# A range test and a guarded general path behind an attention and maxout kernel

## The chip, the cores and the metric

The kernel runs on one core of one Trainium2 chip. The metric is the time of one execution on the device, in microseconds (us). A core has five engines that run side by side, each with its own list of instructions: TensorE (PE in the profile; PEld are its weight loads), VectorE (DVE), ScalarE (ACT), GpSimd (POOL) and SyncE (SP), which issues most DMA transfers. They wait for each other through semaphores.

## The reference

Attention over 8 batches, 8 heads, 1152 keys and 64 dimensions, with queries pooled by two, and behind it a layer of two products whose maximum is taken.

```python
q_pool = q.reshape(B, H, S // 2, 2, D).mean(axis=3)
scores = scale * np.matmul(q_pool, k.transpose(0, 1, 3, 2))
scores = scores - np.max(scores, axis=-1, keepdims=True)
attn = np.exp(scores)
attn = attn / (np.sum(attn, axis=-1, keepdims=True) + 1e-09)
attn_out = np.matmul(attn, v)

x = attn_out.transpose(0, 2, 1, 3).reshape(B * 576, 512)
h1 = x @ w1                       # 512 x 1024
h2 = x @ w2                       # 512 x 1024
out = np.maximum(h1, h2) @ w_out  # 1024 x 512
```

q, k and v are drawn from a normal distribution times 0.1.

## The kernel before

The work is cut into 32 pairs of heads (four pairs a batch). For each pair, q, k and v are loaded in fp32 and cast to bf16 (GpSimd), q and k are transposed, and TensorE makes the scores in groups of 2 x 512 columns into PSUM. ScalarE takes the exponential without subtracting a row maximum and writes `et` in bf16. TensorE multiplies by v, which carries a column of ones, so that column 64 of each result holds the softmax sum. `norm` (line 517) takes the reciprocals of those sums on VectorE, into one of two small tiles `rc` (five columns for the first head of a pair, four for the second), and multiplies the results by them (lines 521 and 525) into `xnat`. After a transposition the rows stand in `xT`.

The maximum is computed as max(h1 - h2, 0) + h2: the weights' difference `wd` and the product `w21` of w2 and w_out are made once. `h_jobs` multiplies xT by wd, with a maximum with zero on the way out of PSUM (lines 778 and 782); `p_job` sums the products with w21 and w_out (line 864), and the result is copied to `osb` by ScalarE or VectorE in turn (lines 891 and 894; 876 and 880 for the last block, which is cut in two) and stored by SyncE and ScalarE (line 735; `store_pair`, lines 745 and 751, earlier).

A planner lays out all operations with costs, then `reorder` puts the lists of TensorE, VectorE, GpSimd and SyncE into orders that are written out by hand as strings, one letter an operation (`pe_order`, `dve_order`, `pool_order`, `sp_order`). `solve` works out which semaphore each operation waits for: an operation counts up its engine's semaphore only if another needs it. `emit` writes each engine's list in that order (line 197 issues the waits). So an operation that waits holds up everything behind it on its engine.

At the end, SyncE waits for the last stores (line 204), and leaving the block (profile line 249) drains every engine and joins them in a barrier. Nothing follows.

Of the kernel before, what the change touches and what calls it, by code (L numbers as in the profile page):

```python
# [1 line left out]

# [2 lines left out]

FP32 = mybir.dt.float32
BF16 = mybir.dt.bfloat16
P = 128

EXP = mybir.ActivationFunctionType.Exp  # L10
RELU = mybir.ActivationFunctionType.Relu
COPY = mybir.ActivationFunctionType.Copy
ALU = mybir.AluOpType
AX = mybir.AxisListType


class Plan:
# [75 lines left out]
    def lane(self, o):  # L93
        key = (o["w"] or ("o",))[0]
        if o["eng"] == "PE":
            return "S" if key[0] == "s" else key[1:]
        if o["eng"] == "SP":
            return {"kT": "t"}.get(key[:2], key[0])
        if o["eng"] == "POOL":
            return {"kb": "k", "wd": "d"}.get(key[:2], key[0])  # L100
        for k in o["r"] + o["w"]:
            if k[0] == "f" and k[1:].isdigit():
                return k[1:]
        return {"qt": "T", "w2": "W", "wo": "W"}.get(key[:2], "Q")

    def reorder(self, want):

# [37 lines left out]
    def solve(self):  # L145
        ops = self.ops
        know = {}
        dma_seen = {}
        for n, o in enumerate(ops):
            eng = o["eng"]  # L150
            kn = know.setdefault(eng, {})
            o["waits"] = []
            for d in sorted(o["deps"], reverse=True):
                p = ops[d]
                if p["dma"] is None:
                    if p["eng"] == eng and not o["fence"] and (eng == "PE" or eng != "DVE" and d not in o["raw"]):
# [12 lines left out]
            if o["dma"] is not None:  # L169
                dma_seen[o["dma"]] = dma_seen.get(o["dma"], 0) + 1  # L170
                o["count"] = 16 * dma_seen[o["dma"]]
        need = set()
        for o in ops:
            need.update(o["waits"])
        cnt = {}
        for n, o in enumerate(ops):
            if o["dma"] is None:
                o["inc"] = n in need
                if o["inc"]:
                    cnt[o["eng"]] = cnt.get(o["eng"], 0) + 1  # L180
                    o["count"] = cnt[o["eng"]]
        self.dma_total = {k: 16 * v for k, v in dma_seen.items()}
# [30 lines left out]
        self.single = single  # L213


def bass_funnel_attn__then__act_maxout2_kernel(
    nc: bass.Bass,
    q: bass.AP,
# [19 lines left out]
    NC_ = C // P  # L238
    NF = F // P
# [9 lines left out]
    with ctx:  # L249
        def sbuf(shape, dt, name):  # L250
            return ctx.enter_context(nc.sbuf_tensor(name, list(shape), dt))
# [3 lines left out]

        ident = sbuf([P, P], BF16, "ident")
        qraw = [sbuf([P, QU, 2, D], FP32, f"qraw{s}") for s in range(3)]
# [147 lines left out]
        def dve(fn, r, w, cost):  # L405
            op("DVE", fn, r=r, w=w, cost=cost)
# [73 lines left out]
        def av_jobs(i):  # L480
            b, h0 = i // NHP, 2 * (i % NHP)
            es = i % 2
            vs = i % 3
            xs = b % 2
            need = [f"et{es}.{g - first(i)}" for g in range(first(i), after(i))] + [f"vE{vs}", f"v.{i}"]

            def col(half, t, sb):
                return (half * 2 + es) * PW + flat(i, t, sb * P)

            def chunk(half, sb):  # L490

                def go(e, m):
                    for t in range(NT):
                        a = col(half, t, sb)
                        last = e.matmul(  # L495
                            fb[m][:, sb * 66:sb * 66 + 65], et[:, a:a + P],
                            vE[vs][:, t, half, 0:65], start=(t == 0), stop=(t == NT - 1))
                    return last
                return unit(need, 0.2755, go)

            def rest():

                def go(e, m):
                    for t in range(NT):
                        for half in range(2):
                            a = col(half, t, NCH)
                            last = e.matmul(  # L507
                                fb[m][rows(half), NCH * 66:NCH * 66 + 65], et[:, a:a + NB],
                                vE[vs][:, t, half, 0:65], start=(t == 0), stop=(t == NT - 1))
                    return last  # L510
                return unit(need, 0.308, go, "c")

            def norm(half):
                def evac(m):
                    n = NCH + 1 - half
                    a = fb[m][:, 0:(NCH + 1) * 66].rearrange("p (j c) -> p j c", c=66)
                    dve(lambda e: e.reciprocal(rc[half][:, 0:n], a[:, 0:n, 64:65]),  # L517
                        [f"f{m}"], [f"rc{half}"], 0.19)
                    if half == 0:
                        for k in range(2):  # L520
                            dve(lambda e, k=k: e.tensor_tensor(
                                xnat[xs][rows(0), i % NHP, NCH, k * D:k * D + D], a[rows(k), NCH, 0:D],
                                rc[0][rows(k), NCH:NCH + 1].to_broadcast([HP, D]), ALU.mult),
                                [f"f{m}", "rc0"], [f"xr{xs}.{h0 + k}"], 0.221)
                    dve(lambda e: e.tensor_tensor(
                        xnat[xs][:, i % NHP, 0:NCH, half * D:half * D + D], a[:, 0:NCH, 0:D],
                        rc[half][:, 0:NCH].unsqueeze(2).to_broadcast([P, NCH, D]), ALU.mult),
                        [f"f{m}", f"rc{half}"], [f"xn{xs}.{h0 + half}", f"f{m}"], 0.425)
# [847 lines left out]
        while p_end[0] < NTOK:  # L1376
# [69 lines left out]
        plan.solve()  # L1446
        engines, dmas = plan.sems()
        sem = {n: ctx.enter_context(nc.semaphore("sem_" + n)) for n in engines + dmas}
        block = ctx.enter_context(nc.Block())

        @block.gpsimd
        def _(g):
            plan.emit("POOL", g, sem)

        @block.sync
        def _(sp):
            plan.emit("SP", sp, sem, last_waits=[f"d_o{s}" for s in range(4)] + [f"d_z{s}" for s in range(4)])

        @block.vector
        def _(vc):  # L1460
            plan.emit("DVE", vc, sem)

        @block.scalar
        def _(ac):
            plan.emit("ACT", ac, sem)

        @block.tensor
        def _(pe):
            plan.emit("PE", pe, sem)


# [26 lines left out]
```

## Time and profile before

| | |
|---|---|
| median of 3 runs | 367.25 us (365.64 to 368.3) |
| profiled execution | span of 368.9 us, from the first to the last instruction; the page gives no separate time for it |
| TensorE busy | 359.1 us of the span |
| mean granted TensorE clock | 0.984 |
| HBM read, written | 62.91 MB, 9.44 MB |

All times in the profile are of that one execution. A group's row gives the engine's line, the operation, what it writes and reads, the count, then busy time and the mean duration in ns, and behind the second bar the engine's idle time before it and what ended that. A letter q behind an engine's name means its sequencer: waits, branches, drains and DMA issues, which don't count as busy.

### The profile page before, as it was taken

What the parts mean: (1) busy time and instruction counts of PE and PEld (TensorE: products, weight loads), DVE (VectorE), ACT (ScalarE), POOL (GpSimd) and SP (SyncE); (2) the same over time, 40 slices, a digit from 0 to 9 for tenths busy, and PEclk for the clock granted to TensorE, in tenths of its full rate; (3) what the DMA queues carried; (4) which work ended last, traced back from release to release, by engine and by line L of the source; (5) the groups of instructions that cost most, each with busy time, mean ns of one, the idle gap of its engine ahead of it and who ended that gap; (6) DMA issues with size and microseconds to landing.
All of it is one profiled execution on the core that took longest, in us unless ns stands there. A gap on an engine that the chain in (4) does not pass through costs nothing.

```text
span 368.9 us, 13316 instructions
## 1 busy us (share of the span) xinstructions
PE 359.1 (97%) x5941; PEld 225.9 (61%) x5945; DVE 240.9 (65%) x521; ACT 315.6 (86%) x355; POOL 124.7 (34%) x111
## 2 busy tenths in 40 slices
PE   6999999999999999999999999999999999999996
PEld 5766564665556665657565665665666666556853
DVE  1478378867778867848885776577877766714411
ACT  4699989999999998999998999999999989895221
POOL 1256675533134333372242602525224440010000
PEclk9599999999999999999999999999999999999999
DMA  7999959999939998898999999998999680913206
GB/s 265 406 396 397 402 108 328 307 312 164 330 102 234 291 271 253 211 297 178 251 349 185 252 245 236 283 304 181 277 253 197 191 201 6 181 43 72 54 0 171
DMA packets 77640, 84.71 MB, mean 230 GB/s; under 512 B 49936, under 2 KB 50704, under 8 KB 77584
## 3 DMA queue, kind: packets, MB, share of 16 engines
q1 hardware_dynamic: 77024, 83.09, 84.8%
q8 instruction: 46, 0.75, 0.9%
q10 hardware_dynamic: 560, 0.79, 0.6%
q14 instruction: 10, 0.08, 0.1%
HBM read 62.91 MB, written 9.44 MB: 196 GB/s over the span
## 4 chain that ended last, share of the span: by engine, by line
PE 95%; DMA 2%; ACT 2%; issue 1%; SPq 0%; POOL 0%; DVE 0%; DVEq 0%
PE sps L584 22%; PE sps L495 12%; PE sps L831 11%; PE fb L831 10%; PE fb L495 9%; PE sps L798 8%; PE fb L798 7%; PE sps L864 3%; PE sps L507 2%; PE fb L716 2%; DMA kraw<-in_k_dram 2%; ACT et L591 2%; PE fb L507 1%; PE fb L864 1%; PE sps L771 1%; PE fb L319 1%
## 5 line engine op out<-in xcount | busy, mean ns | idle before, releaser
L591 ACT ACTIVATE et<-sps 128x1024 bf16<-128x1024 f32 (+1 forms) x336 | 307.6, 1002 | 25.1 <-PE sps L584 23.0
L584 PE MATMUL sps<-qpT,kT 64*128 64x256 bf16 (+7 forms) x1162 | 121.5, 287 | 1.0 <-issue 0.5
L449 DVE STREAM_TRANSPOSE qpT<-qp 32x288 bf16<-32x288 bf16 x216 | 101.3, 469 | 5.6 <-PE sps L584 1.5
L584 PEld LDWEIGHTS sps<-qpT,kT 64*128 64x128 bf16 x1162 | 49.6, 95 | 48.1 <-ACT et L591 15.8
L389 POOL TENSOR_TENSOR qp<-qraw 128x576 bf16<-128x576 f32 x30 | 42.1, 1406 | 98.2 <-DVE qpT L449 76.2
L395 POOL TENSOR_SCALAR vE<-vraw 128x1152 bf16<-128x1152 f32 x32 | 36.9, 1154 | 60.7 <-DMA vraw<-in_v_dram 60.7
L495 PE MATMUL sps<-vE,et 128*128 128x65 bf16 x1368 | 48.4, 193 | 0.0
L495 PEld LDWEIGHTS sps<-vE,et 128*128 128x128 bf16 x1368 | 43.6, 97 | 6.0 <-issue 5.3
L356 POOL TENSOR_SCALAR kbf<-kraw 128x1152 bf16<-128x1152 f32 x31 | 35.7, 1153 | 33.5 <-DMA kT<-kbf 16.5
L798 PE MATMUL sps<-xT,wd 64*128 64x512 bf16 (+3 forms) x368 | 43.7, 326 | 0.0
L831 PE MATMUL sps<-wo,stage 64*128 64x512 bf16 x256 | 36.8, 376 | 0.0
L495 PE MATMUL fb<-vE,et 128*128 128x65 bf16 x936 | 33.5, 193 | 0.5 <-issue 0.5
L798 PE MATMUL fb<-xT,wd 64*128 64x512 bf16 (+3 forms) x272 | 33.6, 333 | 0.1
L495 PEld LDWEIGHTS fb<-vE,et 128*128 128x128 bf16 x936 | 29.9, 97 | 5.5 <-issue 4.8
L831 PE MATMUL fb<-wo,stage 64*128 64x512 bf16 x224 | 33.0, 376 | 0.0
L807 DVE TENSOR_SCALAR stage<-sps 128x1024 bf16<-128x1024 f32 (+3 forms) x23 | 22.3, 969 | 15.7 <-PE sps L798 15.6
L798 PEld LDWEIGHTS sps<-xT,wd 64*128 64x128 bf16 x368 | 15.6, 94 | 13.7 <-PE sps L798 1.4
L807 DVE TENSOR_SCALAR stage<-fb 128x1024 bf16<-128x1024 f32 (+3 forms) x17 | 17.0, 999 | 10.7 <-PE fb L798 10.4
L517 DVE RECIPROCAL rc<-sps 128x5 f32<-128x5 f32 (+1 forms) x38 | 7.1, 186 | 19.7 <-PE sps L495 19.2
L831 PE MATMUL sps<-w,xT 64*128 64x512 bf16 x128 | 18.7, 377 | 0.0
L842 DVE COPY stage<-sps 128x1024 f32<-128x1024 f32 x8 | 9.8, 1225 | 12.8 <-PE sps L831 12.7
L831 PEld LDWEIGHTS sps<-wo,stage 64*128 64x128 bf16 x256 | 12.1, 94 | 9.5
(81 smaller groups left out, 296.6 us busy)
## 6 DMA issues: line engine op xcount, KB each, us to landing
vraw<-in_v_dram SPq DMA_DIRECT2D x32, 576.0 KB, 6.6
kraw<-in_k_dram SPq DMA_DIRECT2D x31, 576.0 KB, 6.6
qraw<-in_q_dram SPq DMA_DIRECT2D x31, 576.0 KB, 6.7
out_dram<-stage SPq DMA_DIRECT2D x21, 256.0 KB, 5.5
out_dram<-stage SPq DMA_DIRECT2D x23, 128.0 KB, 3.2
xT<-in_moe_w_dram SPq DMA_DIRECT2D x4, 512.0 KB, 10.7
stage<-in_moe_w_out_dram SPq DMA_DIRECT2D x4, 512.0 KB, 13.5
stage<-in_moe_w_dram SPq DMA_DIRECT2D x4, 512.0 KB, 13.1
```

Source lines behind the costliest of these rows:

```text
L356: op("POOL", lambda g: g.tensor_scalar(kbf[s][:, :, :, :].rearrange("p t h d -> p h t d"), kraw[r][:, :, :, :], 1.0, 1.0, ALU.mult, ALU.mu ...
L389: op("POOL", lambda g: g.tensor_tensor(qpf[s][:, :, :], qraw[r][:, :, 0, :], qraw[r][:, :, 1, :], ALU.add), r=[f"qraw{r}"], w=[f"qp{s}.0", ...
L395: op("POOL", lambda g: g.tensor_scalar(vE[r][:, :, :, 0:D].rearrange("p t h d -> p h t d"), vraw[r][:, :, :, :], 1.0, 1.0, ALU.mult, ALU.m ...
L449: op("DVE", lambda e: e.transpose(view[dst:dst + 32, :, 32 * pb:32 * pb + 32], qpf[s][src:src + 32, :, 32 * db:32 * db + 32]), r=[f"qp{s}. ...
L495: last = e.matmul(fb[m][:, sb * 66:sb * 66 + 65], et[:, a:a + P], vE[vs][:, t, half, 0:65], start=(t == 0), stop=(t == NT - 1))
L507: last = e.matmul(fb[m][rows(half), NCH * 66:NCH * 66 + 65], et[:, a:a + NB], vE[vs][:, t, half, 0:65], start=(t == 0), stop=(t == NT - 1))
L584: last = e.matmul(sps[r][:, h, col:col + hi - lo], kT[i % 3][rows(h), t, :], qpT[i % 3][rows(h), lo:hi], start=True, stop=True)
L591: op("ACT", lambda e: e.activation(et2[:, :, c:c + z - a], sps[r][:, :, a - g * W:z - g * W], EXP, scale=scale), r=[f"s{r}"], w=keys + ([f ...
L798: last = e.matmul(fb[m + k][:, 0:size], wd[z, ct, (f0 + k) * P:(f0 + k + 1) * P], xT[z, ct, n0:n1], start=(turn == 0 and ct == 0), stop=(t ...
L807: dve(lambda e: e.tensor_scalar_max(gT[:, f0:f0 + 2, g0:g0 + size], wide[m // 2][:, :, 0:size], 0.0), [f"f{m}", f"f{m + 1}"], w + [f"f{m}" ...
L831: last = e.matmul(fb[m + k][:, :], lhs, rhs, start=(turn == 0 and j == 0), stop=(turn == 1 and j == NC_ + NF - 1))
L864: return e.matmul(fb[m][:, 0:c1 - c0], lhs, rhs[:, c0:c1], start=(j == 0), stop=(j == NC_ + NF - 1))
```

## The change

It has four parts.

1. The reciprocals of all softmax sums are kept: `rcs` holds nine columns for each of the 32 pairs, in place of the two tiles `rc`. Three small tiles (`bad`, `badr`, `flag`) are allocated outside the main block.
2. Five operations on VectorE and one DMA transfer on SyncE test the range. Two reductions take the largest and the smallest of the 288 reciprocals of each partition; two operations on one column compare them with the limits 1e18 and 1e-18; the transfer gathers the 128 results into one partition; a last reduction makes one integer of them, `flag`. In `dve_order` the five stand together (`GGGGG`) ahead of the last three operations, the two copies of line 894 and that of line 880; in `sp_order` the transfer (`g`) stands ahead of the last seven stores.
3. Behind its own list, each of the five engines waits until `flag` is written and loads it into a register. On SyncE this comes ahead of the wait for the last stores.
4. Behind the closing barrier, `guarded` puts the general path into a branch that is taken if the register isn't zero: attention in fp32 with the row maximum subtracted, in a loop over batches with the eight heads unrolled, then the maxout layer in fp32 in a loop over 36 blocks of rows. It writes `out` anew.

```diff
+SUM_LO, SUM_HI = 1.0 / 1e18, 1e18
...
-                o["inc"] = n in need
+                o["inc"] = n in need or "gd4" in o["w"]
...
+def guarded(nc, taken, q, k, v, w1, w2, wo, out):
+    B, H, S, D = q.shape
...
+    with nc.If_ne(taken, 0):
+        with TileContext(nc) as tc:
...
+                with tc.For_i(0, B, 1) as b:
+                    for h in range(H):
+                        softmax_head(nc, pool, ps, ident, q, k, v, out, b, h, scale)
+        with TileContext(nc) as tc:
...
+                with tc.For_i(0, B * SQ // P, 1) as n:
+                    maxout(nc, pool, ps, ident, wt, out, n, NC_, NF)
+
+
+def softmax_head(nc, pool, ps, ident, q, k, v, out, b, h, scale):
+    B, H, S, D = q.shape
+    SQ, NT = S // 2, S // P
+    T3 = NT // 3
...
+    for t in range(NT):
+        tp = ps.tile([P, P], FP32, name="tp")
+        nc.tensor.matmul(tp[0:D, :], kf[:, t, :], ident[:, :], start=True, stop=True)
+        nc.vector.tensor_copy(kT[:, t, :], tp[0:D, :])
+    for lo in range(0, SQ, P):
+        n = min(P, SQ - lo)
...
+        nc.tensor.matmul(tq[0:D, 0:n], qs[0:n, :], ident[0:n, 0:n], start=True, stop=True)
...
+        for c in range(3):
+            nc.tensor.matmul(sc[0:n, c, 0:T3 * P], qT[:, 0:n],
+                             kT[:, c * T3:c * T3 + T3, :].rearrange("d t p -> d (t p)"), start=True, stop=True)
...
+        nc.vector.tensor_reduce(top[0:n, :], sc[0:n, :, 0:T3 * P], AX.XY, ALU.max)
...
+        nc.scalar.activation(ex[0:n, :, :], sc[0:n, :, 0:T3 * P], EXP, bias=low[0:n, 0:1], scale=scale)
...
+        for t in range(NT):
+            te = ps.tile([P, P], FP32, name="tp")
+            nc.tensor.matmul(te[:, 0:n], ex[0:n, t // T3, (t % T3) * P:(t % T3) * P + P], ident[0:n, 0:n],
+                             start=True, stop=True)
+            nc.vector.tensor_copy(eT[:, t, 0:n], te[:, 0:n])
...
+        for t in range(NT):
+            nc.tensor.matmul(av[0:n, :], eT[:, t, 0:n], vf[:, t, :], start=(t == 0), stop=(t == NT - 1))
...
+        nc.sync.dma_start(out[bass.ds(b * SQ + lo, n), h * D:h * D + D], ao[0:n, :])
+
+
+def maxout(nc, pool, ps, ident, wt, out, n, NC_, NF):
...
+    for f in range(NF):
+        a = ps.tile([P, P], FP32, name="ha")
+        for c in range(NC_):
+            nc.tensor.matmul(a[:, :], w1[:, c, f * P:f * P + P], xT[:, c, :], start=(c == 0), stop=(c == NC_ - 1))
...
+        for c in range(NC_):
+            nc.tensor.matmul(z[:, :], w2[:, c, f * P:f * P + P], xT[:, c, :], start=(c == 0), stop=(c == NC_ - 1))
+        nc.vector.tensor_tensor(g[:, f, :], z[:, :], first[:, :], ALU.max)
...
+    for f in range(NF):
+        nc.tensor.matmul(y[:, :], g[:, f, :], wo[:, f, :], start=(f == 0), stop=(f == NF - 1))
...
+    outer = ExitStack()
+    bad = outer.enter_context(nc.sbuf_tensor("bad", [P, 4], FP32))
+    badr = outer.enter_context(nc.sbuf_tensor("badr", [1, P], FP32))
+    flag = outer.enter_context(nc.sbuf_tensor("flag", [1, 1], I32))
...
-        rc = [sbuf([P, NCH + 1], FP32, f"rc{s}") for s in range(2)]
+        rcs = sbuf([P, NPAIR, 2 * NCH + 1], FP32, "rcs")
...
-                    dve(lambda e: e.reciprocal(rc[half][:, 0:n], a[:, 0:n, 64:65]),
+                    dve(lambda e: e.reciprocal(rcs[:, i, half * (NCH + 1):half * (NCH + 1) + n], a[:, 0:n, 64]),
...
+        allrc = rcs[:, :, :].rearrange("p i c -> p (i c)")
+        dve(lambda e: e.tensor_reduce(bad[:, 0:1], allrc, AX.X, ALU.max), ["rc0", "rc1"], ["gd0"], 0.4)
+        dve(lambda e: e.tensor_reduce(bad[:, 1:2], allrc, AX.X, ALU.min), ["rc0", "rc1"], ["gd1"], 0.4)
+        dve(lambda e: e.tensor_scalar(bad[:, 2:3], bad[:, 0:1], 1.0 / SUM_LO, 1.0, ALU.is_gt, ALU.mult),
+            ["gd0"], ["gd2"], 0.1)
+        dve(lambda e: e.scalar_tensor_tensor(bad[:, 3:4], bad[:, 1:2], 1.0 / SUM_HI, bad[:, 2:3],
+                                             ALU.is_lt, ALU.max), ["gd1", "gd2"], ["gd3"], 0.1)
+        op("SP", lambda e: e.dma_start(badr[0:1, :], bad[:, 3:4]), r=["gd3"], w=["gr"], dma="d_g")
+        dve(lambda e: e.tensor_reduce(flag[0:1, 0:1], badr[0:1, :], AX.X, ALU.max), ["gr"], ["gd4"], 0.2)
...
-            "TTT6666770T666667706666770302026025170026")
+            "TTT6666770T666667706666770302026025170GGGGG026")
...
-            "xqxxkvxktxootxxootxoovoooxoxxoxoooooooo")
+            "xqxxkvxktxootxxootxoovoooxoxxoxogooooooo")
...
+        taken = nc.alloc_registers("taken")
+        sure = [o["count"] for o in plan.ops if "gd4" in o["w"]][0]
+
+        def run(name, h):
+            plan.emit(name, h, sem)
+            h.wait_ge(sem["DVE"], sure)
+            h.reg_load(taken[h.engine], flag[0:1, 0:1])
...
-            plan.emit("SP", sp, sem, last_waits=[f"d_o{s}" for s in range(4)] + [f"d_z{s}" for s in range(4)])
+            run("SP", sp)
+            plan.emit("-", sp, sem, last_waits=[f"d_o{s}" for s in range(4)] + [f"d_z{s}" for s in range(4)])
...
+    with outer:
+        guarded(nc, taken, q, k, v, moe_w1, moe_w2, moe_w_out, out)
```

More of the change, by code (lines that the diff above doesn't have):

```diff
@@ L4 @@
 from concourse import mybir
+from concourse.tile import TileContext
 FP32 = mybir.dt.float32
+I32 = mybir.dt.int32
 BF16 = mybir.dt.bfloat16
 P = 128
+SUM_LO, SUM_HI = 1.0 / 1e18, 1e18
 EXP = mybir.ActivationFunctionType.Exp
@@ L103, in lane @@
                 return k[1:]
[L104 removed]
+        return {"qt": "T", "w2": "W", "wo": "W", "gd": "G"}.get(key[:2], "Q")
     def reorder(self, want):
@@ L213, in __init__ @@
         self.single = single
+def guarded(nc, taken, q, k, v, w1, w2, wo, out):
+    B, H, S, D = q.shape
+    C, F = w1.shape
+    SQ, NT, NC_, NF = S // 2, S // P, C // P, F // P
+    scale = 0.5 / float(D) ** 0.5
+    with nc.If_ne(taken, 0):
+        with TileContext(nc) as tc:
+            with ExitStack() as st:
+                pool = st.enter_context(tc.tile_pool(name="sp", bufs=1))
+                ps = st.enter_context(tc.tile_pool(name="pp", bufs=1, space=bass.MemoryType.PSUM))
+                ident = pool.tile([P, P], FP32, name="idf")
+                nc.gpsimd.memset(ident[:, :], 1.0)
+                nc.gpsimd.affine_select(
+                    ident[:, :], ident[:, :], pattern=[[1, P]], compare_op=ALU.is_equal,
+                    fill=0.0, base=0, channel_multiplier=-1)
+                with tc.For_i(0, B, 1) as b:
+                    for h in range(H):
+                        softmax_head(nc, pool, ps, ident, q, k, v, out, b, h, scale)
+        with TileContext(nc) as tc:
+            with ExitStack() as st:
+                pool = st.enter_context(tc.tile_pool(name="sm", bufs=1))
+                ps = st.enter_context(tc.tile_pool(name="pm", bufs=1, space=bass.MemoryType.PSUM))
+                ident = pool.tile([P, P], FP32, name="idm")
+                nc.gpsimd.memset(ident[:, :], 1.0)
+                nc.gpsimd.affine_select(
+                    ident[:, :], ident[:, :], pattern=[[1, P]], compare_op=ALU.is_equal,
+                    fill=0.0, base=0, channel_multiplier=-1)
+                wt = []
+                for name, w, n in (("w1", w1, NC_), ("w2", w2, NC_), ("wo", wo, NF)):
+                    t = pool.tile([P, n, w.shape[1]], FP32, name=name + "s")
+                    nc.sync.dma_start(t[:, :, :], w.rearrange("(c p) f -> p c f", p=P))
+                    wt.append(t)
+                with tc.For_i(0, B * SQ // P, 1) as n:
+                    maxout(nc, pool, ps, ident, wt, out, n, NC_, NF)
@@ new lines, in softmax_head @@
+def softmax_head(nc, pool, ps, ident, q, k, v, out, b, h, scale):
+    B, H, S, D = q.shape
+    SQ, NT = S // 2, S // P
+    T3 = NT // 3
+    kf = pool.tile([P, NT, D], FP32, name="kf")
+    vf = pool.tile([P, NT, D], FP32, name="vf")
+    kT = pool.tile([D, NT, P], FP32, name="kTf")
+    nc.sync.dma_start(kf[:, :, :], k[bass.ds(b, 1), h, :, :].rearrange("b (p t) d -> (b p) t d", t=NT))
+    nc.sync.dma_start(vf[:, :, :], v[bass.ds(b, 1), h, :, :].rearrange("b (p t) d -> (b p) t d", t=NT))
+    for t in range(NT):
[4 more added lines that the diff above has]
+        n = min(P, SQ - lo)
+        qf = pool.tile([P, 2, D], FP32, name="qf")
+        nc.sync.dma_start(
+            qf[0:n, :, :],
+            q[bass.ds(b, 1), h, 2 * lo:2 * lo + 2 * n, :].rearrange("b (p r) d -> (b p) r d", r=2))
+        qs = pool.tile([P, D], FP32, name="qs")
+        nc.vector.tensor_tensor(qs[0:n, :], qf[0:n, 0, :], qf[0:n, 1, :], ALU.add)
+        tq = ps.tile([P, P], FP32, name="tp")
+        nc.tensor.matmul(tq[0:D, 0:n], qs[0:n, :], ident[0:n, 0:n], start=True, stop=True)
+        qT = pool.tile([D, P], FP32, name="qTf")
+        nc.vector.tensor_copy(qT[:, 0:n], tq[0:D, 0:n])
+        sc = ps.tile([P, 3, 512], FP32, name="sc")
+        for c in range(3):
+            nc.tensor.matmul(sc[0:n, c, 0:T3 * P], qT[:, 0:n],
+                             kT[:, c * T3:c * T3 + T3, :].rearrange("d t p -> d (t p)"), start=True, stop=True)
+        top = pool.tile([P, 1], FP32, name="top")
+        nc.vector.tensor_reduce(top[0:n, :], sc[0:n, :, 0:T3 * P], AX.XY, ALU.max)
+        low = pool.tile([P, 1], FP32, name="low")
+        nc.vector.tensor_scalar(low[0:n, :], top[0:n, :], -scale, 1.0, ALU.mult, ALU.mult)
+        ex = pool.tile([P, 3, T3 * P], FP32, name="ex")
+        nc.scalar.activation(ex[0:n, :, :], sc[0:n, :, 0:T3 * P], EXP, bias=low[0:n, 0:1], scale=scale)
+        tot = pool.tile([P, 1], FP32, name="tot")
+        nc.vector.tensor_reduce(tot[0:n, :], ex[0:n, :, :], AX.XY, ALU.add)
+        den = pool.tile([P, 1], FP32, name="den")
+        nc.vector.tensor_scalar(den[0:n, :], tot[0:n, :], 1e-9, 1.0, ALU.add, ALU.mult)
+        inv = pool.tile([P, 1], FP32, name="inv")
+        nc.vector.reciprocal(inv[0:n, :], den[0:n, :])
+        eT = pool.tile([P, NT, P], FP32, name="eT")
+        for t in range(NT):
[3 more added lines that the diff above has]
+            nc.vector.tensor_copy(eT[:, t, 0:n], te[:, 0:n])
+        av = ps.tile([P, D], FP32, name="av")
+        for t in range(NT):
+            nc.tensor.matmul(av[0:n, :], eT[:, t, 0:n], vf[:, t, :], start=(t == 0), stop=(t == NT - 1))
+        ao = pool.tile([P, D], FP32, name="ao")
+        nc.vector.tensor_tensor(ao[0:n, :], av[0:n, :], inv[0:n, 0:1].to_broadcast([n, D]), ALU.mult)
+        nc.sync.dma_start(out[bass.ds(b * SQ + lo, n), h * D:h * D + D], ao[0:n, :])
@@ new lines, in maxout @@
+def maxout(nc, pool, ps, ident, wt, out, n, NC_, NF):
+    w1, w2, wo = wt
+    x = pool.tile([P, NC_ * P], FP32, name="x")
+    nc.sync.dma_start(x[:, :], out[bass.ds(n * P, P), :])
+    xT = pool.tile([P, NC_, P], FP32, name="xTf")
+    for c in range(NC_):
+        tx = ps.tile([P, P], FP32, name="tx")
+        nc.tensor.matmul(tx[:, :], x[:, c * P:c * P + P], ident[:, :], start=True, stop=True)
+        nc.vector.tensor_copy(xT[:, c, :], tx[:, :])
+    g = pool.tile([P, NF, P], FP32, name="g")
+    for f in range(NF):
+        a = ps.tile([P, P], FP32, name="ha")
+        for c in range(NC_):
+            nc.tensor.matmul(a[:, :], w1[:, c, f * P:f * P + P], xT[:, c, :], start=(c == 0), stop=(c == NC_ - 1))
+        first = pool.tile([P, P], FP32, name="first")
+        nc.vector.tensor_copy(first[:, :], a[:, :])
+        z = ps.tile([P, P], FP32, name="hz")
+        for c in range(NC_):
+            nc.tensor.matmul(z[:, :], w2[:, c, f * P:f * P + P], xT[:, c, :], start=(c == 0), stop=(c == NC_ - 1))
+        nc.vector.tensor_tensor(g[:, f, :], z[:, :], first[:, :], ALU.max)
+    y = ps.tile([P, NC_ * P], FP32, name="y")
+    for f in range(NF):
+        nc.tensor.matmul(y[:, :], g[:, f, :], wo[:, f, :], start=(f == 0), stop=(f == NF - 1))
+    o = pool.tile([P, NC_ * P], FP32, name="o")
+    nc.vector.tensor_copy(o[:, :], y[:, :])
+    nc.sync.dma_start(out[bass.ds(n * P, P), :], o[:, :])
@@ L522, in evac @@
                                 xnat[xs][rows(0), i % NHP, NCH, k * D:k * D + D], a[rows(k), NCH, 0:D],
-                                rc[0][rows(k), NCH:NCH + 1].to_broadcast([HP, D]), ALU.mult),
+                                rcs[rows(k), i, NCH:NCH + 1].to_broadcast([HP, D]), ALU.mult),
                                 [f"f{m}", "rc0"], [f"xr{xs}.{h0 + k}"], 0.221)
@@ L1452, in _ @@
         def _(g):
-            plan.emit("POOL", g, sem)
+            run("POOL", g)
         @block.sync
         def _(sp):
-            plan.emit("SP", sp, sem, last_waits=[f"d_o{s}" for s in range(4)] + [f"d_z{s}" for s in range(4)])
+            run("SP", sp)
+            plan.emit("-", sp, sem, last_waits=[f"d_o{s}" for s in range(4)] + [f"d_z{s}" for s in range(4)])
         @block.vector
         def _(vc):
-            plan.emit("DVE", vc, sem)
+            run("DVE", vc)
         @block.scalar
         def _(ac):
-            plan.emit("ACT", ac, sem)
+            run("ACT", ac)
         @block.tensor
         def _(pe):
-            plan.emit("PE", pe, sem)
+            run("PE", pe)
+    with outer:
+        guarded(nc, taken, q, k, v, moe_w1, moe_w2, moe_w_out, out)
 _INS = ['q', 'k', 'v', 'moe_w1', 'moe_w2', 'moe_w_out']
```

2 lines of the change are left out of this document (1 added, 1 removed).

## The prediction

> **What bounds the kernel now.** I read the page first: shares of the engines, then the chain that ended last.
>
> ```profile
> span 368.9 us, 13316 instructions
> PE 359.1 (97%) x5941; PEld 225.9 (61%) x5945; DVE 240.9 (65%) x521; ACT 315.6 (86%) x355; POOL 124.7 (34%) x111
> ...
> PE 95%; DMA 2%; ACT 2%; issue 1%; SPq 0%; POOL 0%; DVE 0%; DVEq 0%
> ```
>
> TensorE is busy for 97% of the span and makes 95% of the chain. The change adds no matmul to the path that runs, so it can cost time in three ways: it delays a matmul, it delays the last outputs, or it adds something behind them. What it adds, beside moved storage, is in the last 17 us, so I read that stretch next: the timeline in order of time (start, duration, engine, line; in brackets the idle time before it).
>
> ```profile
> 340.68 0.18 DVE L517 RECIPROCAL rc<-sps 128x4 f32<-128x4 f32 x1
> ...
> 341.24 0.63 SPq L745 DMA_DIRECT2D out_dram<-stage  x1
> ...
> 351.63 0.42 DVE L782 TENSOR_SCALAR stage<-fb 128x256 bf16<-128x256 f32 x1
> ...
> 358.94 7.45 SPq L735 DMA_DIRECT2D out_dram<-stage  x7
> ...
> 359.51 0.69 DVE L894 COPY stage<-fb 128x512 f32<-128x512 f32 x1 [7.46 <-PE fb L864]
> ...
> 362.05 0.69 DVE L894 COPY stage<-sps 128x512 f32<-128x512 f32 x1 [1.84 <-PE sps L864]
> ...
> 365.29 1.39 ACTq L735 DMA_DIRECT2D out_dram<-stage  x2
> 365.42 0.29 DVE L880 COPY stage<-sps 128x128 f32<-128x128 f32 x1 [2.67 <-PE sps L864]
> ```
>
> VectorE is idle for 7.46 us between the L782 evacuation that ends at 351.63 + 0.42 = 352.05 and the L894 copy at 359.51. SyncE issues nothing from 341.24 + 0.63 = 341.87 to 358.94. Last, the end itself: the lines that wait for the outputs (L204) and close the block (L249), and SyncE's waits.
>
> ```profile
> L204 SPq EVENT_SEMAPHORE  x4: 17/28/28, 368.2 to 368.4; - x4
> ```
> ```profile
> L249 DVEq DRAIN  x1: 305/305/305, 365.5 to 365.5; - x1
> L249 ACTq DRAIN  x1: 397/397/397, 366.7 to 366.7; - x1
> L249 SPq COMPARE_BRANCH  x1: 41/41/41, 368.5 to 368.5; - x1
> L249 SPq DRAIN  x1: 7/7/7, 368.7 to 368.7; - x1
> ...
> L249 PEldq EVENT_SEMAPHORE  x1: 51/51/51, 368.8 to 368.8; - x1
> ```
> ```profile
> SPq L735 <- ACT stage L891: 19.1, 3, 17.1
> SPq L204 <- DMA out_dram<-stage: 1.8, 1, 1.8
> ```
>
> The outputs' landing releases SyncE at 368.2, SyncE's branch and drain follow, and the barrier ends the span. All other engines have drained well before that.
>
> **The change, part by part.**
>
> Moved storage. The 64 reciprocals write into one array of 32 x 9 columns in place of two small tiles; their number, shapes and ordering keys are as before.
>
> ```profile
> L517 DVE RECIPROCAL rc<-sps x38: 165/189/198, 46.1 to 340.7; 128x5 f32<-128x5 f32 x19, 128x4 f32<-128x4 f32 x19
> L517 DVE RECIPROCAL rc<-fb x26: 142/184/197, 24.9 to 298.7; 128x5 f32<-128x5 f32 x13, 128x4 f32<-128x4 f32 x13
> ```
>
> If each became slower or faster by the whole spread of its row (0.03 us below the median, 0.01 above), that is 64 x 0.03 = 1.9 us less or 0.6 us more on an engine with 35% idle time, spread over 316 us. I take nothing: TensorE's 95% of the chain hides it.
>
> Two reductions over 128x288. The nearest rows by operation and by size:
>
> ```profile
> L669 DVE TENSOR_REDUCE xT<-xT 128x1024 bf16<-128x1024 f32 x4 | 4.8, 1208 | 0.0
> ...
> L782 DVE TENSOR_SCALAR stage<-sps 128x256 bf16<-128x256 f32 x4 | 1.7, 424 | 2.6 <-PE sps L771 2.6
> ...
> L782 DVE TENSOR_SCALAR stage<-sps 128x128 bf16<-128x128 f32 x3 | 0.9, 288 | 1.3 <-PE sps L771 1.3
> ```
>
> From 128 to 256 elements costs 0.136 us, so 288 cost 0.424 + 32 x 0.136 / 128 = 0.46 us; the reduction's own row by proportion gives 1.208 x 288 / 1024 = 0.34. I take 0.46 each, 0.92 for both. The two one-element operations behind them lie between nothing and a small reciprocal (0.19); I take 0.19 each. Each step waits for the one before it; a semaphore instruction costs 0.017 to 0.051 us on the rows of L204 and L249, so four make at most 0.2. The sum: 0.92 + 0.38 + 0.2 = 1.5 us. The input has been complete since 340.9 (the last reciprocal), so the range word is ready at 352.05 + 1.5 = 353.55.
>
> The gather of 128 words into one row, on SyncE. It is placed ahead of the seven L735 stores, in the gap where the wait of 17.1 us stands in SyncE's list. No four-byte transfer is in the trace; the bounds are the last stores and the transposes, which move two-byte elements:
>
> ```profile
> DMA to landing us min/median/max: 2.2/2.4/3.0
> ```
> ```profile
> xT<-xnat SPq DMA_TRANSPOSE x48, 4.3
> ```
>
> I take 2.4, the median of L735, and keep 2.2 and 4.3. It lands at 353.55 + 2.4 = 355.95 (355.75 to 357.85). The last reduction over 128 elements costs 0.29 by its row, so the flag stands at 356.3 (356.0 to 358.2).
>
> What queues behind: on VectorE, which waits for the gather in order, the L894, L894 and L880 copies, and behind them their stores on SyncE and ScalarE. The cover is 359.51 - 356.3 = 3.2 us (1.3 at the slow end). If the cover is gone, the delay first eats the idle 1.84 and 2.67 us ahead of the later copies: the end moves only when the flag is later than 365.42 - 2 x 0.69 = 364.0. On SyncE one more issue (0.63 at L745) falls into its 17 us. Cost: nothing.
>
> The wait and the register load on five engines. TensorE, GpSimd and VectorE end early (VectorE's drain is at 365.5). ScalarE ends its last issue at 365.29 + 1.39 = 366.7, drains for 0.4 and must be there when SyncE drains at 368.7: slack 368.7 - 367.1 = 1.6. SyncE ends its last issue at 358.94 + 7.45 = 366.4, and the load comes before its wait for the outputs, which ends at 368.2: slack 1.8. No register load is in the trace. Bounds: 0.02, a semaphore instruction, and 2.2, the fastest landing from memory; at 2.2 SyncE is late by 0.4 and ScalarE by 0.6, one of which shows, since both feed the same barrier. A load moves one word, which is nearer to a semaphore instruction than to a store of 32 KB or more, so I take a value under 1.6: nothing, and keep 0 to 0.6. The Trainium skill, page "Runtime: NRT & Kernel Launch", section "Instruction fetch mechanics", puts a register load at about 200 ns; by that, as an estimate, the sum is also nothing.
>
> The branch behind the barrier. Every engine compares its register and jumps over the general path. The row is SyncE's COMPARE_BRANCH: 0.04 us, and 0.2 to the next instruction (368.5 to 368.7). I take the upper one, since this branch is taken: +0.2, bounds 0.04 and 0.2 without a fetch.
>
> Sum: 0 (storage) + 0 (range test) + 0 (gather and flag) + 0 (loads) + 0.2 (branch) = +0.2 us; nothing is removed, so no part can gain: 368.9 becomes 369.1. The page gives the span and no separate time of that execution; the span is 1.65 us above the median of the three runs and 0.6 above the slowest. On the median's scale the forecast is 367.25 + 0.2 = 367.45, rounded 367.5.
>
> **The rivals.**
>
> Far jump (slower). The code of five engines does not lie ready; it comes by DMA in blocks:
>
> ```profile
> q8 instruction: 46, 0.75, 0.9%
> q10 hardware_dynamic: 560, 0.79, 0.6%
> q14 instruction: 10, 0.08, 0.1%
> ```
>
> 0.75 MB in 46 packets is 16 KB each; TensorE's 5941 + 5945 instructions over 46 blocks are 258 to a block. The general path is unrolled over eight heads: 8 x (9 + 5 x (1 + 3 + 9 + 9)) = 952 matmuls in its first half alone, nearly four blocks. The jump's target therefore isn't in the next block, and the engine must stand until it is fetched. The price from the nearest row, a small transfer's landing, is 2.2 us: 369.5. If the target's block and the one behind it are fetched in turn, or a fetch takes as long as the transposes, it is 4.3 to 4.4: 371.7, which is over 1%. This decides if anything that is timed stands behind the jump. For it: TensorE's 46 blocks came without showing in its chain (issue 1%), so straight code is fetched ahead of need; a jump out of the line has no such cover. Against it: in the trace of before the closing barrier is the last record, and behind the jump the program has no work left. The Trainium skill, the same page and section, says that a taken branch whose target lies outside the two-block window forces a DMA fetch before execution goes on; the trace shows the blocks but no far jump, so no run so far shows the stall.
>
> Late gather. If 128 four-byte writes into one partition went through few of the DMA engines, the flag could come after 364.0, that is 10 us behind the range word. A gather of 14 us would end the last copy's wait at 353.55 + 14 + 0.29 + 2 x 0.69 = 369.2 in place of 365.4: +3.8, or 371.1. Against it: the queues move nothing in that stretch (last column, GB/s).
>
> ```profile
> 352.00:359.00 7.00, 7.00 (x36) 3.28 (x35) 0.05 (x1) 1.75 (x5) 0.00 (x0) 1.00 0.00 0
> ```
>
> The flag is set, so the change does other than it says. The price, by the shortest common matmul:
>
> ```profile
> L495 PE MATMUL sps<-vE,et 128*128 128x65 bf16 x1368 | 48.4, 193 | 0.0
> ```
>
> The first half of the general path alone has 64 x 119 matmuls, at 0.193 us over 1.4 ms. Against it: all nine columns of a pair are written (128x5 and 128x4 in the rows of L517), and sums of 1152 terms near one give reciprocals near 0.0009, far inside the limits.
>
> A shift without a place: all later tiles move in on-chip memory and the code behind the block is fetched ahead during the tail. No row prices it; it could go either way by the run-to-run spread (365.64 to 368.3, 0.7%).
>
> **How the numbers follow.** Sum as worked out: 0.46. Far jump, one fetch: 0.24; long form, over 1%: 0.17. Late gather: 0.04, half of it over 1%. Flag set: 0.02. Shift: 0.04 faster by over 1%, 0.03 slower. One per cent (3.7 us) is about what a measurement of this kernel can tell from no change. Faster 0.04; within it 0.46 + 0.24 + 0.02 = 0.72; slower 0.17 + 0.02 + 0.02 + 0.03 = 0.24. The range reaches from the quiet case with the lower part of the run spread, 367.5 - 1.3 = 366.2, to the long form, 371.7, rounded 371.8; it leaves out some 0.2: faster, flag, shift and the tails.
>
> **What would show it.** Right: five new VectorE operations between 352 and 357; a gather that lands before 358; the L894 copy at its old distance from its matmul; register loads on ScalarE and SyncE that end before 368; branches of 0.04 to 0.2 us as the last records. Wrong: a gap of 2 us or more behind a COMPARE_BRANCH, a SyncE wait that ends on a register load, or a first L894 copy released by the flag's reduction in place of TensorE. A longer TensorE stretch before 352 would mean the shift.

## The result, and the profile after

The changed kernel takes 370.23 us (median of 7 runs, 369.36 to 371.3) against 367.25 before: a ratio of 1.0086, 95% interval 1.0059 to 1.0113. That is 3 us more, inside the stated range and, by its middle value, inside 1% (the interval reaches just past it), but 2.7 us over the predicted 367.5, which had next to nothing for the change.

The tail first: VectorE in order of time, from the last evacuation ahead of the range test to the last copy.

```profile
346.72 0.42 DVE L908 TENSOR_SCALAR stage<-fb 128x256 bf16<-128x256 f32 x1
347.06 0.44 DVE L1540 TENSOR_REDUCE bad<-rcs 128x1 f32<-128x288 f32 x1
347.42 0.44 DVE L1541 TENSOR_REDUCE bad<-rcs 128x1 f32<-128x288 f32 x1
347.78 0.14 DVE L1542 TENSOR_SCALAR bad<-bad 128x1 f32<-128x1 f32 x1
347.96 0.16 DVE L1544 SCALAR_TENSOR_TENSOR bad<-bad 128x1 f32<-128x1 f32 x1
350.13 0.27 DVE L1547 TENSOR_REDUCE flag<-badr 1x1 int32<-1x128 f32 x1 [2.02 <-DMA badr<-bad]
354.61 0.69 DVE L1020 COPY stage<-fb 128x512 f32<-128x512 f32 x1 [4.20 <-PE fb L990]
357.14 0.69 DVE L1020 COPY stage<-sps 128x512 f32<-128x512 f32 x1 [1.84 <-PE sps L990]
360.51 0.29 DVE L1006 COPY stage<-sps 128x128 f32<-128x128 f32 x1 [2.67 <-PE sps L990]
```

The gap that was 7.46 us now holds the range test, and 4.20 us of it are left. The three copies behind it (L894, L894 and L880 before) stand as far from each other as they did, and TensorE still releases them: nothing here is late. The register loads, by their line:

```profile
L1591 POOLq TENSOR_LOAD <-flag x1: 487/487/487, 350.4 to 350.4; - x1
L1591 PEldq TENSOR_LOAD <-flag x1: 636/636/636, 358.6 to 358.6; - x1
L1591 DVEq TENSOR_LOAD <-flag x1: 627/627/627, 360.5 to 360.5; - x1
L1591 SPq TENSOR_LOAD <-flag x1: 830/830/830, 361.5 to 361.5; - x1
L1591 ACTq TENSOR_LOAD <-flag x1: 720/720/720, 361.8 to 361.8; - x1
```

They end by 362.5, more than a microsecond ahead of the barrier's end. The barrier's last record and then the branch on each engine (it carries a line of the library, bacc.py:44):

```profile
L375 PEldq EVENT_SEMAPHORE  x1: 51/51/51, 363.9 to 363.9; - x1
```
```profile
bacc.py:44 POOLq COMPARE_BRANCH  x1: 45/45/45, 363.9 to 363.9; - x1
bacc.py:44 SPq COMPARE_BRANCH  x1: 54/54/54, 363.9 to 363.9; - x1
bacc.py:44 ACTq COMPARE_BRANCH  x1: 54/54/54, 363.9 to 363.9; - x1
bacc.py:44 DVEq COMPARE_BRANCH  x1: 72/72/72, 364.0 to 364.0; - x1
bacc.py:44 PEldq COMPARE_BRANCH  x1: 3649/3649/3649, 364.0 to 364.0; - x1
```

Four engines branch in 45 to 72 ns. TensorE's branch takes 3649 ns and ends the span. The DMA view of that stretch alone (363.95 to 367.7) shows what moves meanwhile: code, one packet of 16 KB on TensorE's queue (q8) and four of 8 KB on the queue that the other four engines' code comes by (q14).

```profile
q14 instruction: 4, 0.03, 3.2%
q8 instruction: 1, 0.02, 1.6%
```

One caution on the two spans. The execution profiled before has 368.9 us, the one after 367.7, although the kernel became slower. The clock row shows why: the one before ran its second slice, near the start, at half clock, and the one after didn't.

```profile
PEclk9599999999999999999999999999999999999999
```
```profile
PEclk9999999999999999999999999999999999999997
```

Aligned at the end of the closing barrier, before stands at 368.9 and after at 363.9: these five microseconds lie ahead of the branch, where the run without a branch (below) shows no price of the change. The first experiment gives the spans that belong to the times.

### The profile page after: what moved, and what is told of

It is laid out like the page before. It is cut to its first block, busy times and chain, and to the rows that moved or that the text cites. A ratio compares the mean times of both kernels' runs of the same rounds, so it can differ in the third digit from the quotient of the medians.

```text
span 367.7 us, 13340 instructions
## 1 busy us (share of the span) xinstructions
PE 354.8 (96%) x5945; PEld 222.7 (61%) x5945; DVE 242.1 (66%) x526; ACT 315.0 (86%) x355; POOL 124.7 (34%) x111
## 4 chain that ended last, share of the span: by engine, by line
PE 92%; DMA 2%; ACT 2%; SPq 1%; issue 1%; DVE 0%; DVEq 0%
PE sps L710 21%; PE sps L621 12%; PE sps L957 11%; PE fb L957 10%; PE fb L621 9%; PE sps L924 8%; PE fb L924 7%; PE sps L990 3%; DMA qraw<-in_q_dram 2%; PE sps L633 2%; PE fb L842 2%; ACT et L717 2%; PE fb L633 2%; PE fb L990 1%; PE sps L897 1%; PE fb L897 1%
## 5 line engine op out<-in xcount | busy, mean ns | idle before, releaser
L710 PE MATMUL sps<-qpT,kT 64*128 64x256 bf16 (+7 forms) x1162 | 118.2, 283 | 0.6 <-ACT et L717 0.3
L710 PEld LDWEIGHTS sps<-qpT,kT 64*128 64x128 bf16 x1162 | 47.9, 94 | 47.9 <-ACT et L717 15.8
L643 DVE RECIPROCAL rcs<-sps 128x5 f32<-128x5 f32 (+1 forms) x38 | 7.0, 185 | 19.8 <-PE sps L621 19.3
```

Source lines behind the costliest of these rows:

```text
L710: last = e.matmul(sps[r][:, h, col:col + hi - lo], kT[i % 3][rows(h), t, :], qpT[i % 3][rows(h), lo:hi], start=True, stop=True)
```

## The experiments

Theory 1: all of the added time is the jump over the general path, whose target an engine has to fetch while it stands still (its stand, below). Each ratio below is against runs of the kernel before on the same chip. Instructions that an engine jumps over are counted in its compiled list.

**The kernel before, once more.** No edit.

> The kernel before, once more, to have its span beside its time. Both theories: ratio 1.000 (0.997 to 1.003). In the seven runs of the changed kernel the time was 1.5 to 2.1 us above the span; if the same holds here, a time of 365.6 to 367.3 goes with a span of 363.9 to 365.6, and the execution profiled before the change (span 368.9, half clock for 10 us near its start) was a long one by about 5 us.

366.06 us, ratio 0.9988 (0.9968 to 1.0009). Over its 12 runs the span's median is 364.25 and the time less the span 1.69 to 1.87 us, once 2.6; in the seven runs of the changed kernel it is 1.5 to 2.1 on a median span of 368.7. So time is span and some 1.75 us for both, and the difference of the kernels lies inside the span. The execution profiled here has a span of 367.6 at full clock, so a single one can lie 3 us off its median without the clock.

**No branch.**

```diff
-    with outer:
-        guarded(nc, taken, q, k, v, moe_w1, moe_w2, moe_w_out, out)
+    outer.close()
```

> Range test, gather, flag, waits and register loads as in the change, but no branch and no general path behind the barrier. Theory 1 (all of the time is the jump over the general path, 3.65 us in TensorE's COMPARE_BRANCH): 367.25 to 367.6, ratio 0.998 to 1.002. Rival 1 (the added tail or the moved tiles cost it): 369.5 to 370.5, ratio 1.006 to 1.010. Between the two: both share it.

366.27 us, ratio 1.0001 (0.9979 to 1.0023). Moved tiles, range test, gather and the waits for the flag cost nothing that can be measured, and rival 1 falls. With it falls the prediction's shift without a place, for all that stands ahead of the branch. One thing differs from what was meant: without a reader of the register the compiled program has no register loads; its trace shows none. The next run has them.

**A short general path.**

```diff
-                with tc.For_i(0, B, 1) as b:
...
-                    maxout(nc, pool, ps, ident, wt, out, n, NC_, NF)
```

> The branch stays, but the general path behind it is cut to the making of one identity tile (TensorE jumps over some 9 instructions, not 4173). Leaves the general path's loops out. Theory 1 (a block of code has to be fetched): the target is already there, TensorE's COMPARE_BRANCH takes under 0.2 us, time 367.3 to 367.8, ratio 1.000 to 1.003. Rival 2 (every taken branch costs it, whatever lies between): COMPARE_BRANCH 3 to 4 us and 370, ratio 1.008.

367.01 us, ratio 1.001 (0.9986 to 1.0033). The loads are there, and the branch too; TensorE's record of it:

```profile
bacc.py:44 PEldq COMPARE_BRANCH  x1: 344/344/344, 364.2 to 364.2; - x1
```

344 ns instead of 3649 (the 0.2 expected was short). A taken branch by itself is not the price: rival 2 falls.

**Heads in a loop.**

```diff
-                    for h in range(H):
+                    with tc.For_i(0, H, 1) as h:
                         softmax_head(nc, pool, ps, ident, q, k, v, out, b, h, scale)
...
```

> The eight heads of the general path in a loop instead of unrolled: TensorE jumps over some 865 instructions instead of 4173, still more than three blocks of 256. Theory 1 with one fetch whatever the distance: COMPARE_BRANCH 3 to 4 us on TensorE and 370, ratio 1.007 to 1.010. Rival 3 (the price grows with the distance): 3.65 x 865 / 4173 = 0.8 us, time 368.0, ratio 1.002.

370.1 us, ratio 1.0115 (1.0086 to 1.0144), a little above what was expected, and TensorE's branch:

```profile
bacc.py:44 PEldq COMPARE_BRANCH  x1: 3829/3829/3829, 364.1 to 364.1; - x1
```

A jump over 865 instructions costs what one over 4173 does. Rival 3, a price by distance, falls.

**Only TensorE's path long.** The short path with matmuls in it:

```diff
...
+                jp = ps.tile([P, P], FP32, name="jp")
+                for _ in range(1000):
+                    nc.tensor.matmul(jp[:, :], ident[:, :], ident[:, :], start=True, stop=True)
```

> The short branch behind the barrier with 1000 fp32 matmuls in it: TensorE jumps over some 4010 instructions, the other engines over 9 to 16. Leaves the general path out. Theory 1: TensorE alone gives the whole of the change: COMPARE_BRANCH 3 to 4 us, 369.7 to 370.7, ratio 1.008 to 1.011, time less span 1.6 to 2.1 us as in the change. Rival 7 (the change's price needs the fetches of several engines at once, which hold each other up): 368 to 369, ratio 1.003 to 1.006.

369.83 us, ratio 1.008 (1.0051 to 1.0108), the change's own ratio, with 1.6 to 2.0 us between span and time.

```profile
bacc.py:44 PEldq COMPARE_BRANCH  x1: 3789/3789/3789, 367.4 to 367.4; - x1
```

During this branch (367.2 to 371.2) nothing moves but one packet on TensorE's queue:

```profile
q8 instruction: 1, 0.02, 1.5%
```

TensorE alone is enough; rival 7 falls. In the short path (363.5 to 364.5) no code moves until TensorE's branch is over; a packet on q8 comes at 365.0, behind the last record, and the time of that execution stays 1.65 us above its span.

**Only VectorE's path long.**

```diff
...
+                for _ in range(890):
+                    nc.vector.memset(ident[0:1, 0:1], 1.0)
```

> The short branch of the second experiment with 890 one-element operations of VectorE put into it: VectorE jumps over some 899 instructions (894 in the change), TensorE over 9. Leaves the general path out. Theory 1 in its narrow form (TensorE alone is what shows): VectorE's fetch takes 8 KB, not 16, and costs at most 1.6 us behind its branch: 366.5 to 368.2, ratio 1.000 to 1.005. Rival 5 (any engine's far jump costs the same): 370, ratio 1.008 to 1.011.

369.12 us, ratio 1.0051 (1.0028 to 1.0075): well under TensorE's price, and at the edge of what theory 1 in its narrow form said (1.005), so the ratio alone doesn't decide. Where the price lies is the instructive part. In the profiled execution no record became long:

```profile
bacc.py:44 DVEq COMPARE_BRANCH  x1: 72/72/72, 364.9 to 364.9; - x1
bacc.py:44 PEldq COMPARE_BRANCH  x1: 350/350/350, 365.0 to 365.0; - x1
```

but the time is 4.0 to 4.3 us above the span in all 12 runs, against some 1.75 in the runs so far: 2.4 us, behind the last record, and more than the 1.6 that theory 1 allowed. The DMA records go on there (365.3 to 369.4):

```profile
q14 instruction: 3, 0.02, 2.1%
q8 instruction: 1, 0.02, 1.6%
```

One 8 KB block comes at 365.9, a microsecond behind VectorE's branch, the next at 368.3. The kernel before and the run without a branch have no code behind their last record. So theory 1 had to be widened: every engine whose target is not loaded stands. On TensorE the stand is inside the branch's record, on VectorE it follows it; by this theory TensorE's 3.65 us cover the others' in the changed kernel, which its trace can't show apart.

**The general path rolled up further.** Loops over heads, pieces of 64 rows and column blocks; TensorE jumps over 328 instructions, the other engines over 120 to 179.

```diff
...
-    for lo in range(0, SQ, P):
-        n = min(P, SQ - lo)
+    n = P // 2
+    with tc.For_i(0, SQ // n, 1) as u:
...
-    for f in range(NF):
+    with tc.For_i(0, NF, 1) as f:
+        c1 = pool.tile([P, NC_, P], FP32, name="c1")
+        nc.vector.tensor_copy(c1[:, :, :], w1[:, :, bass.ds(f * P, P)])
...
```

> Branch behind the barrier as in the change, but the general path rolled up further (loops over heads, over 64-row pieces and over column blocks): TensorE jumps over 328 instructions, 1.3 blocks of 256. Theory 1: all or nothing, since a block is there or not: either COMPARE_BRANCH under 0.4 us and 366.5 to 367.0 (ratio 1.000 to 1.003), or 3 to 4 us and 370 (ratio 1.008 to 1.011), nothing between; the edge lies between one and two blocks. Rival 3 (a price by distance) gave 0.8 us for 865 instructions and would give 0.3 here.

370.44 us, ratio 1.008 (1.0054 to 1.0107). The branch in the profiled execution:

```profile
bacc.py:44 PEldq COMPARE_BRANCH  x1: 470/470/470, 365.7 to 365.7; - x1
```

TensorE's record shows no stand in that execution, yet its time is 5.0 us above its span: neither of the two outcomes that were expected. In the eight others, time less span is 1.6 to 2.1 and the spans are 366.6 to 369.5. In the profiled one the price is thus behind the last record, as with VectorE. From 366.1 to 367.2 the trace has four blocks on q14 and one on q8, as in the changed kernel, then none until 370.3; which engine stood isn't shown. In the other eight the price looks to be inside the span again, for which there is no trace. Where TensorE's edge lies between 9 and 865 instructions stays open. The rolled path bought nothing.

**The jump ahead of the barrier.** Each engine branches as soon as its own list is done; the general path begins with a wait for the stores and a barrier of its own.

```diff
...
-        block = ctx.enter_context(nc.Block())
...
+        for name, h in (("POOL", nc.gpsimd), ("SP", nc.sync), ("DVE", nc.vector), ("ACT", nc.scalar), ("PE", nc.tensor)):
+            run(name, h)
...
     with nc.If_ne(taken, 0):
+        stored()
+        nc.all_engine_barrier()
...
+        guarded(nc, taken, q, k, v, moe_w1, moe_w2, moe_w_out, out, stored)
+        stored()
+        nc.all_engine_barrier()
```

> The same range test, general path and branch, but the branch stands ahead of the closing barrier: each engine jumps as soon as its own list is done, and SyncE waits for the last stores behind its jump (in the general path there is a wait for the stores and a barrier of its own first). Theory 1 (TensorE's fetch of some 3.7 us is the price, and nothing else): TensorE jumps some 4.5 us before the barrier, so its fetch is covered; ScalarE and SyncE jump about 1.3 us before it and may show up to 0.7 us. Time 366.5 to 367.2, ratio 1.000 to 1.002, COMPARE_BRANCH on TensorE still 3 to 4 us long. Rival 4 (the price is not TensorE's fetch but the branch on all engines together, or work of the close that has to follow it): 370, ratio 1.008 to 1.011.

368.94 us, ratio 1.0052 (1.0022 to 1.0082): less than the change's 1.0086, though the two intervals overlap; not what theory 1 said, and not rival 4 either. The branch's line (L1601, where SyncE's waits for the stores, behind its jump, also stand) and the drains of the barrier (L1606):

```profile
L1601 SPq EVENT_SEMAPHORE  x4: 28/28/28, 367.4 to 367.7; - x4
L1601 POOLq COMPARE_BRANCH  x1: 45/45/45, 351.6 to 351.6; - x1
L1601 PEldq COMPARE_BRANCH  x1: 4052/4052/4052, 359.9 to 359.9; - x1
L1601 DVEq COMPARE_BRANCH  x1: 72/72/72, 361.9 to 361.9; - x1
L1601 SPq COMPARE_BRANCH  x1: 58/58/58, 363.9 to 363.9; - x1
```
```profile
L1606 POOLq DRAIN  x1: 107/107/107, 352.0 to 352.0; - x1
L1606 PEldq DRAIN  x1: 73/73/73, 364.0 to 364.0; - x1
...
L1606 DVEq DRAIN  x1: 57/57/57, 364.9 to 364.9; - x1
L1606 SPq DRAIN  x1: 13/13/13, 367.7 to 367.7; - x1
```

TensorE stands for 4.05 us and drains at 364.0, under the stores. VectorE goes from its branch at 361.9 to its drain at 364.9. SyncE jumps last, over 464 instructions, at 363.9, and its next instruction comes at 367.4: 3.5 us in the open. The widened theory predicted that only SyncE's jump has to be shortened.

**The same, with the general path's transfers on GpSimd.** All seven `nc.sync.dma_start` of the general path become `nc.gpsimd.dma_start`.

> The early jump once more, with the general path's transfers issued by GpSimd instead of SyncE, so that SyncE jumps over some 65 instructions instead of 464. In the early jump SyncE branched at 363.9 and went on at 367.4, while TensorE's 4.05 us and VectorE's 2.9 us lay under the stores. Theory 1, widened to every engine (each engine whose target is not loaded stands about 3 to 4 us; only what reaches past the barrier shows): SyncE goes on within 0.5 us, and 366.5 to 367.8, ratio 0.999 to 1.003. Rival 6 (jumping ahead of the barrier costs something of its own, such as fetches against the last stores): 368.5 to 369.2, ratio 1.004 to 1.007, as in the early jump before.

367.14 us, ratio 1.0013 (0.9992 to 1.0034): the whole change, and no measurable price. The same two lines:

```profile
L1601 SPq EVENT_SEMAPHORE  x4: 28/28/517, 363.8 to 364.9; - x4
L1601 POOLq COMPARE_BRANCH  x1: 45/45/45, 351.6 to 351.6; - x1
L1601 PEldq COMPARE_BRANCH  x1: 3809/3809/3809, 359.9 to 359.9; - x1
L1601 DVEq COMPARE_BRANCH  x1: 72/72/72, 361.8 to 361.8; - x1
L1601 SPq COMPARE_BRANCH  x1: 58/58/58, 363.6 to 363.6; - x1
```
```profile
L1606 POOLq DRAIN  x1: 122/122/122, 354.1 to 354.1; - x1
L1606 PEldq DRAIN  x1: 74/74/74, 363.8 to 363.8; - x1
...
L1606 SPq DRAIN  x1: 13/13/13, 364.9 to 364.9; - x1
L1606 DVEq DRAIN  x1: 57/57/57, 364.9 to 364.9; - x1
```

TensorE's branch is as long as ever, 3.8 us. It is under the last stores now, SyncE goes on 0.2 us behind its branch, and VectorE drains together with SyncE. GpSimd, which now has the transfers to jump over, branches at 351.6 in both runs and drains 2.5 us behind that, where it took 0.4 before: the stand has moved to an engine that nobody waits for. Rival 6 falls.

**The flag forced.** The upper limit on the sums at 1.0 sets the flag on these inputs, in the rolled kernel and in the one just told.

```diff
-SUM_LO, SUM_HI = 1.0 / 1e18, 1e18
+SUM_LO, SUM_HI = 1.0 / 1e18, 1.0
```

> The rolled kernel with the upper limit on the sums set to 1.0, so that the flag is set on these inputs and the general path runs. All theories: no statement on the jump; the flag decides, and the time is over 1.4 ms by the prediction's bound (64 x 119 matmuls at 0.193 us), likely some 10 ms.

> The early jump with GpSimd's transfers and the upper limit on the sums at 1.0, so that the general path runs. All theories: no statement on the jump; over 1.4 ms, and by the rolled kernel's 16.9 ms some 10 to 30 ms.

16938 us and 8557 us, from a single execution each. The general path runs when the flag says so, so in all other runs it was jumped over. The estimate of over 1.4 ms was a bound and no more than that, and the second time lies below the 10 to 30 ms expected of it.

## Why the prediction was right, and where it was wrong

The range and the class held because one rival was kept in them: the far jump, one fetch, with a chance of 0.24 and 369.5 us. The likeliest case failed. That the class held is in part luck: the 3.0 us that came were the rival's, not the sum's, and the interval of the ratio reaches 1.0113. Point by point:

**Storage: nothing.** Right, shown by the run without a branch, as far as its interval of some 0.8 us either way goes.

**Range test: 1.5 us, hidden.** Right in kind. From 347.06 to 348.12 it took 1.06: the reductions 0.44 each as forecast (0.46), but the one-element operations 0.14 and 0.16 instead of 0.19, and waits between dependent steps too short to see.

**Gather: 2.4 us, bounds 2.2 to 4.3, and a cover of 3.2.** It landed 2.0 us after its issue, just under the lower bound; the cover left was 4.20. The late gather did not come.

**Register loads: under 1.6, hidden.** Right, within the spread of the run with the short path: 0.49 to 0.83 us, against bounds of 0.02 and 2.2. The figure that the Trainium skill gives ("Runtime: NRT & Kernel Launch", "Instruction fetch mechanics": about 200 ns a register) is a quarter to two fifths of what these loads from on-chip memory took. SyncE's wait for the stores shows the cover shrinking, from 1.8 us to 0.9:

```profile
SPq L207 <- DMA out_dram<-stage: 0.9, 1, 0.9
```

**Branch: +0.2.** Wrong, and this is the step that failed. The row it was read from, SyncE's branch at L249, is a branch that didn't stand: the next record comes 0.2 us later. The rival's mechanism was named and then discounted with the sentence that behind the jump the program has no work left. That missed where the stand is booked: TensorE's own COMPARE_BRANCH record holds it, so it needs no work behind it to be timed, and where the record doesn't hold it (VectorE), the time still does, behind the span. The rival's size was off as well: 2.2 us, from a small transfer's landing, against 3.65 to 4.05 measured. The long form, two fetches in turn for 4.4, was nearer to that record, but the stretch has a single packet on TensorE's queue; the time itself, 3.0 us more with an interval of 2.2 to 4.1, lies between the two. The distance was underestimated too, without consequence: the prediction counted 952 matmuls, nearly four blocks, in the first half, and the whole path has 4173 instructions of TensorE, some 16 blocks.

The Trainium skill ("Runtime: NRT & Kernel Launch", "Instruction fetch mechanics") says that a taken branch out of the two-block window forces a fetch, and gives no size for the stall. The traces agree with that rule as far as they go: TensorE's jump over 9 instructions cost 0.34 us, those over 865, 4010 and 4173 cost 3.65 to 3.83. The 328 instructions of the rolled path, 1.3 blocks, don't decide it.

**The scale.** The prediction took the profiled span as 1.65 us above the median of the times. In truth the time is some 1.75 us above the span of the same execution; the profiled one was a long one, with 10 us at half clock. That error cancelled, since only differences were used. Three smaller slips changed nothing: the spread below the median is 0.04 us in the second row of L517, not 0.03; the flag's time adds up to 356.24, not 356.3; and 371.7 doesn't round to 371.8.

What would make the forecast wrong was listed as a gap of 2 us or more behind a COMPARE_BRANCH. It came inside the record on TensorE, and as a gap on VectorE and SyncE.

## What to carry to other kernels

Code that isn't run can still cost the jump over it. Ask for each engine whether the target of its jump is likely to be loaded, beside what the flag and the test in front cost: here a jump over 9 of TensorE's or 65 of SyncE's instructions went on at once, one over 865 or 464 did not. In this kernel the branch cost nothing measurable once it stood ahead of the closing barrier and under the last transfers, where the engines were done early; put the transfers of the rarely run path on an engine that finishes early, so that the one that finishes last has little to jump over. And compare times with times: two profiled spans may differ by more than the change, and a stand may lie behind the last record.

## What the runs showed of the hardware

A jump to code that isn't loaded stood TensorE for 3.65 to 4.05 us in five profiled executions, VectorE for 2.9 to 3.1 in two (361.9 or 361.8 to 364.9), SyncE for 3.5 and GpSimd for 2.5 (351.6 to 354.1) in one each. Most of it is not the block's transfer. In the changed kernel the transfer takes about a microsecond of the 3.65: the busy share of the 16 DMA engines by stretches (the second number from the right),

```profile
363.95:365.20 1.25, 0.00 (x0) 0.00 (x0) 0.00 (x0) 0.00 (x0) 0.00 (x0) 0.50 0.10 26
365.20:366.30 1.10, 0.00 (x0) 0.00 (x0) 0.00 (x0) 0.00 (x0) 0.00 (x0) 0.50 0.06 15
366.30:367.70 1.40, 0.00 (x0) 0.00 (x0) 0.00 (x0) 0.00 (x0) 0.00 (x0) 0.50 0.00 0
```

has the other engines' blocks in the first stretch, one engine of 16 busy (0.06) for TensorE's 16 KB in the second, and nothing in the 1.4 us before the branch ends. What fills the time ahead of and behind the transfer isn't shown.
